# RWKV-6 attention and a SoLU feed-forward on one core: v and w_in loaded in bf16 by rounding transfers from GpSimd's queue, and a new order

## The chip, the core and the metric

The kernel runs on one core of a Trainium2 chip. The core has a matrix engine (TensorE, PE in the profile), VectorE (DVE), ScalarE (ACT), GpSimd (POOL, called Pool here) and SyncE (SP), which only issues transfers. Transfers are carried out by 16 engines that all queues share. The metric is the time of one execution on the device in microseconds, over several runs; the profile shows one execution more closely.

## The reference

Four sequences of 768 tokens, eight heads of 48 channels. The attention keeps a state of 48 by 48 per head, which decays by w at each token; its output goes through a feed-forward part with 1,024 hidden channels.

```python
for t in range(S):
    cur = einsum('bhd,bhe->bhde', u[None] * k_t, v_t)
    y[:, :, t] = einsum('bhd,bhde->bhe', r_t, state + cur)
    state = w_t[:, :, :, None] * state + einsum('bhd,bhe->bhde', k_t, v_t)
x = y.transpose(0, 2, 1, 3).reshape(B * S, H * D)          # 3072 x 384
h = x @ w_in                                               # 3072 x 1024
solu = h * softmax(h)
ln = (solu - mean(solu)) / sqrt(var(solu) + 1e-6) * g_ln
out = ln @ w_out                                           # 3072 x 384
```

All inputs and the output are float32.

## The kernel before

A unit is 128 tokens of one sequence: six chunks of four sequences, 24 units, numbered so that the four sequences of a chunk follow one another. Each unit passes through the same stages, and the whole program is written out by the string `ORDER`: each word is a stage, the unit's number and, after a dot, the engine or the PSUM slot (`LV3.a`: load v of unit 3 from ScalarE's queue; `kr5.d`: copy by VectorE). Every engine issues its own instructions in the order of these words; the class `InOrder` holds them to it. All its calls go through one line, so nearly every row of the profile carries L89 and is told apart by its tile.

The stages of a unit, by the words of `ORDER`, with the tile's name in the profile:

- Loads of w, k, r, v (`LW`, `LK`, `LR`, `LV`): each 128 partitions x 8 heads x 48 float32, 192 KB, in pieces of 192 bytes. Rings of seven buffers take w, k, r and v as float32. `LI` and `LO` load w_in (three parts of 512 KB) and w_out (two of 768 KB), `LU` and `LG` the vectors u and g.
- Decays: logarithm of w (`lw`, ScalarE), two cumulative products by triangular constants (`cum`, TensorE, tile cum_ps), exponent (`ex`, ScalarE), scaled k and r (`kp`, VectorE).
- The token's own term: `p` = k r and `q` = p u (Pool), their sum per head `dg` (VectorE), `dv` = v dg (Pool, tile dv). `vb` casts v to bf16, by Pool or ScalarE.
- Attention: k and r transposed (`krk`, `krr`, TensorE, tile kr_ps) and copied (`kr`), scores (`M`, tile m_ps), copied and masked (`m` on VectorE does both; `m` on ScalarE is followed by `sel`, Pool's mask), the attend product (`Y`, tile y_ps: from the state, and from masked scores and v; with `i` it also adds dv through an identity product, with `n` VectorE adds dv in `y`), and the state (`S`, `et`, `st`).
- Feed-forward: y transposed (`X`, `xT`, tile x_ps), hidden product (`H`, 24 products, tile h_ps), `e` = exp(h) (ScalarE), `he` = h e (VectorE), `hq` = he squared, the output product in two parts (`Oa`, `Ob`, tile o_ps: 384 columns and one for the mean in one product, and two single columns for the sum of e and of hq), then the factor from the sums (`sq`, `qm`, `lv`: ScalarE, VectorE, ScalarE), the scaling (`o`) and the store (`out`, SP).
- Once: u spread over the partitions (`us`, `uc`), g turned into a column (`gs`, `gc`), w_in cast to bf16 (`wi`), w_out scaled by g (`gw`) and centred (`mn`, `mc`, `ce`). `hot` are warm-up products without use.

The stages `KD` and `XD` transpose k and r, or y, by a transfer; the order before has none of them. The transfer queues are SP and ScalarE: `queue = {"s": sp, "a": act}`. A load waits in its queue for a free buffer of its ring, and everything behind it in that queue waits too.

Of the kernel before, what the change touches and what calls it, by code (L numbers as in the profile page):

```python
# [21 lines left out]
LW0.a LK0.s LU0.a LR0.s LW1.a LW2.s hot4.s3 LG0.s LK1.s lw0 LV0.a cum0.b0 LR1.s us0.s0 ex0 hot2.s3 uc0 lw1 LV1.s  # L22
p0 kp0 LW3.a LK2.a LR2.s krk0.s3 q0 krr0 cum1.b1 kr0.a hot2.s2 LV2.s LK3.a M0.b0 LR3.s p1 gs0.s1 ex1 m0.d
hot3.s3 LI1.s lw2 q1 dg0 cum2.b0 lw3 hot2.s3 kp1 vb0.p LI0.a S0.s2 dv0 vb1.a dg1 hot1.s3 ex2 Y0.is0 et0 LV3.a
cum3.b1 LI2.s p2 kp2 krk1.s3 gc0 LO0.s ex3 st0 LW4.s krk2.s1 q2 krr1 LO1.s krr2 kp3 kr1.a hot3.s2 dv1 LK4.s
kr2.d y0.a p3 M1.b0 LK5.a S1.s2 dg2 krk3.s3 vb2.a m1.d krr3 et1 wi0.a S2.s0 wi1.p M2.b1 st1 X0.s1 kr3.a m2.d
Y1.is2 LR4.s wi2.p et2 y1.a M3.b0 xT0.d LV4.a X1.s3 q3 m3.d H0.b1 dv2 gw1.a dg3 gw2.d e0 Y2.is2 LW5.s xT1.d
gw3.p st2 H1.b0 y2.a he0 lw4 gw0.a X2.s1 LR5.s e1 gw7.d cum4.b1 gw4.d hot2.s3 gw6.d gw5.d ex4 he1 vb3.p mn0.s3
LW6.s LV5.a dv3 xT2.a LK6.s kp4 S3.s0 mc0 Y3.is2 LR6.s lw5 ce6.d krk4.s1 ce3.d hq0.a cum5.b0 ce4.d krr4 ce2.d
H2.b1 ce7.d ex5 LW7.s ce1.d ce5.d ce0.d y3.a LK7.s p4 kp5 et3 Oa0.s3 lw6 e2 LR7.s kr4.d p5 krk5.s2 cum6.b0 st3  # L30
hq1.a Ob0 vb4.p he2 LW8.s q4 krr5 ex6 S4.s1 LK8.s kr5.d sq0 M4.b1 lw7 Oa1.s0 kp6 et4 m4.a LR8.s X3.s2 qm0 st4
vb5.p M5.b0 xT3.a cum7.b1 dg4 sel4 lv0 krk6.s1 LV6.s Ob1 m5.d ex7 LW9.s dv4 lw8 S5.s2 kp7 o0.a krr6 LK9.s p6
cum8.b0 sq1 et5 Y4.ns3 kr6.d ex8 H3.b1 q5 LV7.s y4.d hq2.a kp8 q6 LR9.s krk7.s1 e3 X4.s3 st5 LW10.s vb6.p M6.b0
krr7 xT4.d Oa2.s2 dg5 m6.a LK10.s qm1 kr7.d dv5 krk8.s3 lv1 Ob2 he3 out0 sel6 o1.a lw9 M7.b0 out1 dg6 S6.s1 sq2
m7.a LV8.s hq3.d krr8 cum9.b1 LR10.s Y5.ns0 vb7.p qm2 kr8.d lv2 H4.b0 p7 LW11.s et6 y5.d ex9 st6 p8 lw10 kp9
LV9.s X5.s3 S7.s0 e4 Oa3.s1 q7 o2.d vb8.a he4 out2 cum10.b1 dv6 xT5.a krk9.s2 et7 LK11.s ex10 Y6.ns3 q8 krr9 st7
LV10.s H5.b0 hq4.a kp10 sel7 LR11.s kr9.a y6.d M8.b1 dg7 LW12.s S8.s0 lw11 m8.d Ob3 dv7 et8 e5 LV11.s vb9.p
krk10.s3 st8 X6.s2 LK12.s p9 M9.b1 he5 xT6.a Y7.ns0 sq3 m9.a krr10 LR12.s S9.s2 dg8 cum11.b0 et9 LW13.s y7.d
H6.b1 lw12 dv8 ex11 kr10.d LK13.s p10 qm3 lv3 kp11 Oa4.s0 LR13.s e6 q9 st9 X7.s3 cum12.b0 LW14.s xT7.a Ob4 he6
p11 ex12 LV12.s krk11.s2 sel9 sq4 Y8.ns3 o3.a kp12 H7.b1 hq5.a out3 vb10.p qm4 y8.d q10 LK14.s lv4 dg9 M10.b0 e7  # L40
Oa5.s1 LR14.s m10.d vb11.p q11 o4.a krr11 LW15.s X8.s3 lw13 dg10 Ob5 p12 xT8.a out4 he7 kr11.a S10.s0 dv9 S11.s3
LV13.s dg11 sq5 hq6.a Y9.ns2 vb12.p qm5 cum13.b0 y9.d dv10 LK15.s H8.b1 et10 ex13 st10 LR15.s et11 lw14 kp13
Oa6.s2 LW16.s e8 hq7.d krk12.s0 lw15 M11.b0 p13 st11 LK16.s Ob6 lv5 he8 o5.a q12 krr12 m11.a Y10.ns3 out5 kr12.d
krk13.s1 cum14.b1 LR16.s y10.d sq6 krr13 sel11 ex14 cum15.b0 LW17.s kr13.d Oa7.s0 ex15 qm6 LV14.s kp14 p14
Y11.ns3 lw16 X9.s1 Ob7 kp15 lv6 dv11 LK17.s vb13.a xT9.d p15 o6.a M12.b1 y11.d M13.b0 m12.a X10.s1 out6 m13.d
krk14.s2 q13 S12.s3 LR17.s hq8.a krr14 H9.b1 dg12 LV15.s vb14.p xT10.d sq7 q14 et12 qm7 st12 LW18.s lv7 krk15.s1
dg13 e9 X11.s3 sel12 H10.b0 o7.d kr14.a out7 he9 dv12 LK18.s Y12.ns0 xT11.a p16 krr15 LR18.s Oa8.s2 e10 y12.d
kr15.d q15 LV16.s cum16.b1 he10 S13.s0 ex16 dv13 Ob8 LV17.s et13 kp16 q16 X12.s3 LW19.s Y13.ns1 sq8 xT12.a st13
M14.b0 vb15.p M15.b1 LK19.s m14.a y13.d krk16.s3 S14.s0 hq9.d krr16 LR19.s m15.a S15.s1 p17 qm8 kr16.d H11.b0
LW20.s et14 dg14 lv8 sel14 st14 et15 LK20.s dg15 H12.b1 e11 vb16.p o8.d sel15 st15 out8 lw17 Oa9.s3 he11 LV18.s  # L50
e12 vb17.p dv14 S16.s0 LV19.s hq10.a he12 Ob9 dv15 LR20.s et16 cum17.b0 st16 q17 Y14.ns2 LV20.s ex17 X13.s1
y14.d M16.b1 sq9 Oa10.s0 lw18 kp17 LW21.s m16.a Y15.ns2 qm9 xT13.d LK21.s cum18.b0 hq11.d lv9 krk17.s1 lw19
H13.b1 LR21.s o9.d p18 vb18.a dg16 ex18 LV21.s y15.d dv16 krr17 e13 Ob10 kp18 LW22.s sel16 X14.s3 hq12.a kr17.d
S17.s2 LK22.s cum19.b0 q18 he13 Oa11.s1 xT14.a LR22.s ex19 p19 X15.s3 lw20 M17.b1 out9 xT15.d Ob11 sq10 kp19
vb20.p m17.a LW23.s q19 Y16.ns3 qm10 dg17 et17 vb19.a cum20.b0 p20 LV22.s y16.d lv10 H14.b1 dg18 sq11 ex20 sel17
LK23.s st17 lw21 o10.d LR23.s Oa12.s3 e14 kp20 dv17 krk18.s2 Ob12 out10 hq13.a p21 qm11 he14 krk19.s0 LV23.s
lv11 krr18 q20 cum21.b0 sq12 o11.d krr19 ex21 H15.b1 p22 qm12 kr18.d out11 lv12 kr19.d vb21.p Oa13.s1 dv18 kp21
# [12 lines left out]
"""  # L70

NIO, NLW, NKP, NWK = 7, 10, 6, 4


class InOrder:


    def __init__(self, tc, engine):
# [18 lines left out]
def kernel(  # L97
# [80 lines left out]
    one_col = consts.tile([C, 2], BF16)  # L178
    dve.memset(one_col, 1.0)
    inv_col = consts.tile([C, 1], BF16)  # L180
    dve.memset(inv_col, 1.0 / RDF)
    ones_row = consts.tile([1, C], F32)
    dve.memset(ones_row, 1.0)

# [371 lines left out]
```

The softmax here doesn't subtract the row's maximum and nothing guards it: scores larger than these inputs give would overflow.

## Time and profile before

| | us |
|---|---|
| median of two runs | 154.74 (154.55 to 154.93) |
| profiled execution | 153.27 |
| its span, first to last instruction | 151.6 |
| busy: TensorE | 137.2 (91%) |
| VectorE | 127.9 (84%) |
| ScalarE | 117.9 (78%) |
| Pool | 94.9 (63%) |
| read from memory, written | 22.03 MB, 4.72 MB |

The span is what the profile covers; the execution is 1.7 us longer. A profile row names the line, the engine, the operation, what is written and read with sizes, the count; then the total busy time in us and the mean of one in ns; then the idle time of the engine ahead of these instructions, and who ended it. Buffer numbers are left out, so vb stands for all ten vb buffers. A matrix product's length is modelled and overlaps the next, so a row's mean is longer than the pace at which products follow each other; the pace is read from the chain. A DMA issue row shows how long the queue held the issuing engine, not how long the bytes took.

### The profile page before, as it was taken

To read this page: it belongs to the slowest core of one execution; us is meant where nothing else is said; L and a number is where in the kernel's file an instruction comes from. 1 tells how busy PE (TensorE), PEld (TensorE's weight loads), DVE (VectorE), ACT (ScalarE), POOL (GpSimd) and SP (SyncE) were. 2 spreads that over 40 slices of the span, in tenths; PEclk is the share of its full clock that TensorE was granted. 3 is DMA by queue.
4 is the path that set the end of the run, shared out by engine and by line. 5 is a ranking of instruction groups with operands and counts; after the bars stand their busy time and mean duration, and the time that the engine had idled before them with its cause. 6 is when DMAs were issued, how large, how long until landed. Compare 5 with 4: busy or idle time off the path is not lost.

```text
span 151.6 us, 5258 instructions
## 1 busy us (share of the span) xinstructions
PE 137.2 (91%) x2156; PEld 106.6 (70%) x2158; DVE 127.9 (84%) x235; ACT 117.9 (78%) x238; POOL 94.9 (63%) x127
## 2 busy tenths in 40 slices
PE   4799787879999997999988999999999999999980
PEld 1145566467788776888777797878887888889650
DVE  5209797999999996999976999999998998688940
ACT  3465766599999997999798688999898997484442
POOL 7484993531879859993849999299847682500000
PEclk9999999999999999999999999999999999999997
DMA  5999999999983999989699999898950111011142
GB/s 110 259 257 334 405 335 255 178 210 188 224 179 121 229 217 193 215 176 241 142 243 208 230 175 232 162 230 193 248 164 6 52 56 52 4 52 56 52 160 104
DMA packets 104825, 27.08 MB, mean 179 GB/s; under 512 B 100313, under 2 KB 104418, under 8 KB 104802
## 3 DMA queue, kind: packets, MB, share of 16 engines
q1 hardware_dynamic: 94256, 24.26, 69.6%
q10 hardware_dynamic: 10546, 2.49, 7.3%
q8 instruction: 17, 0.28, 0.7%
q14 instruction: 6, 0.05, 0.1%
HBM read 22.03 MB, written 4.72 MB: 176 GB/s over the span
## 4 chain that ended last, share of the span: by engine, by line
PE 54%; DMA 12%; SPq 10%; DVE 8%; ACT 6%; POOL 4%; issue 4%; ACTq 0%; POOLq 0%
PE o_ps L89 22%; PE h_ps L89 13%; SPq L89 10%; DMA w_in<-in_w_dram 6%; PE kr_ps L89 4%; PE y_ps L89 4%; DMA kr_in<-in_r_dram 4%; PE s_ps L89 3%; PE cum_ps L89 3%; PE m_ps L89 3%; DMA v_in<-in_v_dram 3%; PE x_ps L89 2%; DVE he L89 1%; POOL m L89 1%; DVE w L89 1%
## 5 line engine op out<-in xcount | busy, mean ns | idle before, releaser
L89 PE MATMUL o_ps<-w,he 128*128 128x385 bf16 x192 | 45.7, 325 | 0.1
L89 PE MATMUL h_ps<-xT,win_sb 128*128 128x128 bf16 x576 | 35.9, 219 | 0.3 <-DVE xT L89 0.3
L89 PEld LDWEIGHTS <-win_sb 128*128 128x128 bf16 x576 | 33.0, 98 | 0.9 <-issue 0.4
L89 PE MATMUL o_ps<-inv_col,e 128*128 128x1 bf16 x192 | 31.7, 165 | 0.0
L89 DVE TENSOR_TENSOR he<-h_ps,e 128x1024 bf16<-128x1024 f32 x24 | 29.1, 1216 | 2.7 <-ACT e L89 2.5
L89 PE MATMUL o_ps<-one_col,hq 128*128 128x1 bf16 x192 | 31.3, 163 | 0.0
L89 ACT ACTIVATE e<-h_ps 128x1024 bf16<-128x1024 f32 x24 | 24.5, 1020 | 4.7 <-PE h_ps L89 4.6
L89 DVE TENSOR_TENSOR kp<-cum_ps,kr_in 128x768 bf16<-128x768 f32 x24 | 22.7, 948 | 5.9 <-ACT cum_ps L89 5.6
L89 PEld LDWEIGHTS <-hq 128*128 128x128 bf16 x192 | 18.5, 96 | 12.8
L89 POOL TENSOR_TENSOR p<-kr_in 128x384 bf16<-128x384 f32 x24 | 24.4, 1018 | 3.7 <-DMA kr_in<-in_r_dram 3.6
L89 POOL TENSOR_TENSOR dv<-vb,dg 128x384 bf16<-128x384 bf16 x24 | 19.8, 830 | 9.6 <-DVE dg L89 7.4
L89 POOL TENSOR_SCALAR_AFFINE_SELECT m<-m 128x1024 bf16<-128x1024 bf16 x15 | 16.8, 1120 | 13.4 <-ACT sq L89 5.8
L89 POOL TENSOR_TENSOR q<-p,u_bc 128x384 bf16<-128x384 bf16 x24 | 21.8, 911 | 1.9 <-ACT u_bc L89 1.7
L89 PEld LDWEIGHTS <-kp 128*128 128x128 bf16 x272 | 17.4, 98 | 6.0 <-DVE kp L89 2.1
L89 ACT ACTIVATE cum_ps<-cum_ps 128x768 f32<-128x768 f32 x24 | 19.2, 802 | 3.0 <-PE cum_ps L89 2.9
L89 PE MATMUL kr_ps<-ident,kp 128*128 128x128 bf16 x192 | 18.0, 222 | 2.3 <-ACT gr L89 0.8
L89 PEld LDWEIGHTS <-he 128*128 128x128 bf16 x192 | 18.4, 96 | 0.9
L89 PEld LDWEIGHTS <-e 128*128 128x128 bf16 x192 | 18.4, 96 | 0.5 <-issue 0.2
L89 ACT ACTIVATE lw<-w_in 128x384 bf16<-128x384 f32 x24 | 12.4, 523 | 4.1 <-DMA w_in<-in_w_dram 4.1
L89 ACT CAST m<-m_ps 128x1024 bf16<-128x1024 f32 x15 | 15.0, 1013 | 0.7 <-PE m_ps L89 0.6
L89 DVE TENSOR_TENSOR m<-m_ps,keep 128x1024 bf16<-128x1024 f32 x9 | 10.9, 1215 | 4.2 <-PE m_ps L89 4.2
L89 ACT ACTIVATE hq<-he 128x1024 bf16<-128x1024 bf16 x13 | 13.7, 1057 | 0.0
(82 smaller groups left out, 262.5 us busy)
## 6 DMA issues: line engine op xcount, KB each, us to landing
kr_in<-in_r_dram SPq DMA_DIRECT2D x24, 192.0 KB, 4.3
out_dram<-o SPq DMA_DIRECT2D x24, 192.0 KB, 3.2
kr_in<-in_k_dram SPq DMA_DIRECT2D x21, 192.0 KB, 3.5
w_in<-in_w_dram SPq DMA_DIRECT2D x21, 192.0 KB, 4.2
v_in<-in_v_dram SPq DMA_DIRECT2D x20, 192.0 KB, 4.1
wout_f<-in_moe_w_out_dram SPq DMA_DIRECT2D x2, 768.0 KB, 7.7
win_f<-in_moe_w_in_dram SPq DMA_DIRECT2D x2, 512.0 KB, 5.1
v_in<-in_v_dram ACTq DMA_DIRECT2D x4, 192.0 KB, 4.2
```

The lines of the kernel that those rows point to most:

```text
L89: made = make(*args, **kwargs)
```

## The change

v and the three parts of w_in are loaded straight into bf16 tiles by transfers that Pool issues; the float32 buffers and the 24 + 3 casts are gone, and vb has rows of 64 as the other loads have. Pool's queue also takes ten of the 24 stores, ScalarE's the left half of the last one. SP issues all other loads but four at the start. In units 20 to 23, k and r, and y, are transposed by transfers that SP issues (`KD`, `XD`). The last unit's exponent, product and square are done in two parts, its three sums are computed ahead of its columns, and its columns in two halves (`Mal`, `Mar`, `Mbl`, `Mbr`) that VectorE and ScalarE scale and two queues store. The constants are filled by VectorE in a stage `pc` that stands behind the first three loads of v; Pool keeps four selections; `keep` is the same tile as `uts`. u is rounded to bf16 ahead of its spread. Ten instead of fifteen masks are Pool's, and two centrings. The words stand in a new order throughout.

```diff
@@ ORDER @@
-LW0.a LK0.s LU0.a LR0.s LW1.a LW2.s hot4.s3 LG0.s LK1.s lw0 LV0.a cum0.b0 LR1.s us0.s0 ex0 hot2.s3 uc0 lw1 LV1.s
-p0 kp0 LW3.a LK2.a LR2.s krk0.s3 q0 krr0 cum1.b1 kr0.a hot2.s2 LV2.s LK3.a M0.b0 LR3.s p1 gs0.s1 ex1 m0.d
-hot3.s3 LI1.s lw2 q1 dg0 cum2.b0 lw3 hot2.s3 kp1 vb0.p LI0.a S0.s2 dv0 vb1.a dg1 hot1.s3 ex2 Y0.is0 et0 LV3.a
-cum3.b1 LI2.s p2 kp2 krk1.s3 gc0 LO0.s ex3 st0 LW4.s krk2.s1 q2 krr1 LO1.s krr2 kp3 kr1.a hot3.s2 dv1 LK4.s
-kr2.d y0.a p3 M1.b0 LK5.a S1.s2 dg2 krk3.s3 vb2.a m1.d krr3 et1 wi0.a S2.s0 wi1.p M2.b1 st1 X0.s1 kr3.a m2.d
-Y1.is2 LR4.s wi2.p et2 y1.a M3.b0 xT0.d LV4.a X1.s3 q3 m3.d H0.b1 dv2 gw1.a dg3 gw2.d e0 Y2.is2 LW5.s xT1.d
-gw3.p st2 H1.b0 y2.a he0 lw4 gw0.a X2.s1 LR5.s e1 gw7.d cum4.b1 gw4.d hot2.s3 gw6.d gw5.d ex4 he1 vb3.p mn0.s3
...
-sq21 qm20 qm21 lv20 Oa23.s2 lv21 o20.d o21.d out20 Ob22 out21 Ob23 sq22 qm22 lv22 sq23 qm23 o22.d lv23 out22
-o23.a out23
+LV0.p LV1.p LV2.p pc0 LW0.s LG0.a LU0.s LK0.a hot5.s3 LW1.s LR0.s LW2.s gs0.s0 LK2.s lw0 ur0 LK1.a cum0.b0
+us0.s3 LR1.a hot1.s2 ex0 LR2.s lw1 LW3.s kp0 p0 uc0 cum1.b1 LK3.s lw2 krk0.s2 q0 ex1 krr0 cum2.b0 hot3.s3 ex2
+kp1 p1 LW4.s kr0.d krk1.s1 q1 LR3.s kp2 M0.b1 p2 dg0 LK4.s lw3 krk2.s3 krr1 m0.d krr2 dv0 kr1.a cum3.b0 LR4.s
+S0.s2 q2 dg1 gc0 Y0.is1 LO0.s lw4 kr2.d LI0.p S1.s0 ex3 cum4.b1 dv1 hot2.s3 LO1.s et0 y0.a kp3 LW5.s ex4 p3 dg2
+M1.b0 LK5.s krk3.s3 st0 LI1.p X0.s1 m1.d S2.s2 LR5.s LI2.p dv2 kp4 M2.b0 krr3 LV3.p kr3.a m2.d xT0.a q3 krk4.s3
+gw0.a krr4 Y1.is1 et1 LV4.p gw1.d kr4.a dg3 M3.b1 m3.d y1.a p4 et2 X1.s3 Y2.ns1 xT1.d M4.b0 q4 st1 m4.a H0.b1
+gw3.d LV5.p y2.d gw2.a st2 H1.b0 e0 dg4 LW6.s gw7.d gw6.d gw4.a gw5.d S3.s3 dv3 he0 e1 X2.s0 mn0.s1 LK6.s sel4
+lw5 he1 xT2.a LR6.s Y3.is2 et3 mc0 dv4 cum5.b1 st3 H2.b0 ex5 LW7.s LV6.p ce3.d ce6.d y3.a ce1.d ce5.d LK7.s lw6
+S4.s0 kp5 p5 e2 X3.s1 Y4.ns3 LR7.s xT3.d ce2.p cum6.b1 hq0.a he2 S5.s2 LW8.s krk5.s1 ce7.p et4 ex6 krr5 y4.d
...
+M22.b0 y21.d M23.b1 m22.a Oa18.s0 m23.d XD21 sq17 hq19.a H20.b0 sel22 qm17 out16 et19 lv17 dv23 st19 Y22.ns1 e20
+Y23.ns3 y22.d Ob18 y23.d o17.a XD22 he20 H21.b1 out17.p XD23 Oa19.s1 e21 H22.b0 sq18 hq20.a he21 Ob19 hq21.d
+Ha23.b1 qm18 sq19 lv18 Oa20.s3 e22 o18.d qm19 out18.p Hb23 ea23 he22 Ob20 eb23 lv19 hq22.d Oa21.s2 sq20 o19.a
+heb23 Oa22.s0 out19 qm20 hqb23.d lv20 hea23 Ob21 hqa23.d Ob22 sq21 qm21 o20.d lv21 Sa23.s1 sq22 out20 qm22 o21.d
+Sb23 lv22 Mar23.s3 sq23 out21 Mal23.s2 qm23 o22.d lv23 Mbr23 Mbl23 out22 or23.d ol23.a outr23 outl23.a
@@ constants and buffers @@
-    v_t = ring("v_in", NIO, [C, H, 64], F32)
-    win_f = consts.tile([128, KM, DF], F32)
+    vb_t = ring("vb", NLW, [C, H, 64], BF16)
+    win_sb = consts.tile([128, KM, DF], BF16)
...
-    dve.memset(warm, 0.0)
     uti_neg = consts.tile([C, C], BF16)
-    pool.memset(uti_neg, -1.0)
-    pool.affine_select(out=uti_neg, in_=uti_neg, compare_op=ALU.is_ge, fill=0.0, base=0,
-                       pattern=[[1, C]], channel_multiplier=-1)
...
-    ones_row = consts.tile([1, C], F32)
+    ones_row = consts.tile([1, C], BF16)
...
-    vb_t = ring("vb", NLW, [C, H, D], BF16)
+    keep = uts
+
+    def constants(i, x):
+        dve.memset(warm, 0.0)
+        dve.memset(uti_neg, -1.0)
+        dve.memset(uts, 1.0)
+        dve.memset(ident, 0.0)
+        dve.memset(ident_f, 0.0)
+        pool.affine_select(out=uti_neg, in_=uti_neg, compare_op=ALU.is_ge, fill=0.0, base=0,
+                           pattern=[[1, C]], channel_multiplier=-1)
...
+        dve.memset(halves, 0.0)
+        dve.memset(off_blocks, 0.0)
+        for row, own in ((0, 0), (32, 1)):
+            dve.memset(halves[row:row + 1, 64 * own:64 * own + 64], 1.0)
+            dve.memset(off_blocks[row:row + 1, :, 1 - own], -30000.0)
...
-    queue = {"s": sp, "a": act}
+    queue = {"s": sp, "a": act, "p": pool}
@@ loads, u and the casts @@
     def load_v(i, x):
-        queue[x].dma_start(out=v_t[i % NIO][:, :, :D], in_=rows_of(v, i))
+        queue[x].dma_start(out=vb_t[i % NLW][:, :, :D], in_=rows_of(v, i))
...
     def load_w_in(j, x):
-        queue[x].dma_start(out=win_f[:, j, :], in_=moe_w_in[j * 128:(j + 1) * 128, :])
+        queue[x].dma_start(out=win_sb[:, j, :], in_=moe_w_in[j * 128:(j + 1) * 128, :])
...
+    def round_u(i, x):
+        dve.tensor_copy(out=u_b, in_=u_row)
+
     def spread_u(i, x):
         ps["u"] = bank([C, DM], F32, x, "u_ps")
-        pe.matmul(ps["u"], lhsT=ones_row, rhs=u_row, start=True, stop=True)
+        pe.matmul(ps["u"], lhsT=ones_row, rhs=u_b, start=True, stop=True)
...
-    def cast_w_in(j, x):
-        copy = {"a": act.copy, "d": dve.tensor_copy, "p": pool.tensor_copy}[x]
-        copy(out=win_sb[:, j, :], in_=win_f[:, j, :])
...
-    def v_cast(i, x):
-        copy = {"a": act.copy, "p": pool.tensor_copy}[x]
-        copy(out=vb_t[i % NLW], in_=v_t[i % NIO][:, :, :D])
@@ the last unit @@
-    def hidden(i, x):
-        xT = xT_t[i % NWK]
-        h_ps = live[i]["h_ps"] = bank([128, KF, C], F32, x, "h_ps")
-        for f in range(KF):
+    def hidden_part(i, f0, f1):
+        xT, h_ps = xT_t[i % NWK], live[i]["h_ps"]
+        for f in range(f0, f1):
             for j in range(KM):
...
+    def hidden_a(i, x):
+        live[i]["h_ps"] = bank([128, KF, C], F32, x, "h_ps")
+        hidden_part(i, 0, KF // 2)
...
+    def hidden_exp(i, x, part=ALL):
+        act.activation(out=e_t[i % NWK][:, part], in_=live[i]["h_ps"][:, part], func=EXP)
...
+    HALF = {"l": slice(0, DM // 2), "r": slice(DM // 2, DM)}
+
+    def columns_of(i, x, side, part):
+        if part == 0:
+            live[i]["o" + side] = bank([C, DM // 2], F32, x, "o_ps")
+        for f in range(part * KF // 2, (part + 1) * KF // 2):
+            pe.matmul(live[i]["o" + side], lhsT=he_t[i % NWK][:, f, :], rhs=w2[:, f, HALF[side]],
+                      start=(f == 0), stop=(f == KF - 1))
+
+    def sums_of(i, x, part):
+        if part == 0:
+            live[i]["sums"] = bank([C, 3], F32, x, "o_ps")
+        to = live[i]["sums"]
+        for f in range(part * KF // 2, (part + 1) * KF // 2):
+            pe.matmul(to[:, 0:1], lhsT=he_t[i % NWK][:, f, :], rhs=w2[:, f, DM:], start=(f == 0), stop=False,
+                      skip_group_check=True)
...
-    def scaled_out(i, x):
-        o_ps, rs, o = live[i]["o_ps"], rs_t[i % NWK], o_t[i % NWK]
+    def scaled_out(i, x, side=""):
+        rs, o = rs_t[i % NWK], o_t[i % NWK][:, HALF.get(side, slice(0, DM))]
...
-    def store(i, x):
+    def store(i, x, side=""):
         c, b = units[i]
-        sp.dma_start(out=out[b * S + c * C:b * S + (c + 1) * C, :], in_=o_t[i % NWK])
+        cols = HALF.get(side, slice(0, DM))
+        queue[x or "s"].dma_start(out=out[b * S + c * C:b * S + (c + 1) * C, cols], in_=o_t[i % NWK][:, cols])
```

## The prediction

> **What bounds the kernel now.** I read the time slices first, then the busy table by stage, then the chain of waits, then the groups. The slices (engine, busy tenths of 40 slices of 3.8 us):
>
> ```profile
> PE   4799787879999997999988999999999999999980
> POOL 7484993531879859993849999299847682500000
> DMA  5999999999983999989699999898950111011142
> ```
>
> Two things overlap: transfers are full until slice 29 (110 us), and TensorE is nearly full from slice 10 (38 us). The stages, cut at the first output product (34 us), the last load (110), Pool's last instruction (131) and TensorE's last (146.4); columns are named in the first line:
>
> ```profile
> core 0: us, PE busy (x) PEld busy (x) DVE busy (x) ACT busy (x) POOL busy (x), PEclk, DMA share, GB/s
> 0.00:34.00 34.00, 26.51 (x269) 15.65 (x272) 23.24 (x57) 20.84 (x38) 21.78 (x41) 1.00 1.07 261
> 34.00:110.00 76.00, 73.54 (x1261) 60.27 (x1259) 71.81 (x120) 68.95 (x141) 59.74 (x71) 1.00 0.96 202
> 110.00:131.00 21.00, 21.00 (x373) 17.55 (x372) 18.57 (x33) 18.52 (x35) 13.41 (x15) 1.00 0.19 59
> 131.00:146.40 15.40, 15.40 (x255) 12.60 (x254) 13.44 (x25) 7.74 (x21) 0.00 (x0) 1.00 0.16 59
> ```
>
> The first 34 us belong to the transfers (share 1.07, TensorE idle 7.5 us and 7.8 us of its busy time are warm-up products, rows of 7.2 and 0.6). After that TensorE sets the pace: idle 2.5 us in 76, then not at all. Pool is free 21% of the middle and ends 20.7 us before the span. The end, from the chain of waits (start, length, what):
>
> ```profile
> 135.65 0.17 PE x_ps L89 x3
> 135.82 0.83 PE o_ps L89 x12
> 136.65 0.19 PE x_ps L89 x3
> 136.84 1.34 PE h_ps L89 x24
> ...
> 140.38 5.98 PE o_ps L89 x84
> 146.38 0.18 ACT sq L89
> ...
> 148.20 0.58 ACT o L89
> ```
>
> These lengths are TensorE's real pace: 1.34 us for a unit's hidden product, 0.83 for half its output product, 0.19 for three transposes; elsewhere in the chain 0.24 for four transposes of k or r. After the last product 5.2 us remain. The rows that the change touches on Pool and ScalarE, and one issue row (ns minimum, median, maximum):
>
> ```profile
> L89 POOL TENSOR_TENSOR p<-kr_in 128x384 bf16<-128x384 f32 x24 | 24.4, 1018 | 3.7 <-DMA kr_in<-in_r_dram 3.6
> L89 POOL TENSOR_TENSOR q<-p,u_bc 128x384 bf16<-128x384 bf16 x24 | 21.8, 911 | 1.9 <-ACT u_bc L89 1.7
> L89 POOL CAST vb<-v_in 128x384 bf16<-128x384 f32 x17 | 8.5, 502 | 6.1 <-DMA v_in<-in_v_dram 6.1
> L89 ACT CAST vb<-v_in 128x384 bf16<-128x384 f32 x7 | 3.6, 515 | 1.4 <-DMA v_in<-in_v_dram 1.3
> L89 ACTq DMA_DIRECT2D v_in<-in_v_dram x4: 374/374/379, 4.3 to 29.9; - x4
> ```
>
> **What the Trainium skill says.** "DMA: Bandwidth & Descriptors", section "SWDGE vs HWDGE vs iDMA": a transfer that changes the type can only be issued by GpSimd, whose own cores then write every descriptor. The trace before has no such transfer. Its section "Latency and other measured facts" gives about 1 us to the first byte on that path, named as the emission overhead, against 0.6 us for the hardware path; the 0.374 us above is the hardware issue alone. "SBUF — State Buffer", section "Who interferes with whom": GpSimd cannot write descriptors while VectorE runs an operation that takes both ports. No run here shows it, but VectorE is 94% busy in the middle. "Issuing engines are not separate DMA queues" (the first page): the bytes still share the same engines, so 1.07 and 0.96 are not relieved by another queue.
>
> **The change part by part.**
> *Casts gone.* 24 casts of v (8.5 us Pool, 3.6 us ScalarE) and three of w_in (2.0 Pool, 1.0 ScalarE). TensorE covers nearly all of it: only one v cast (0.48 us) lies on the chain. Worth at most 1 us.
>
> *Pool's new queue.* c is what one issue holds Pool. 24 loads of v, 3 of w_in and 10 stores make 37 issues, 35 ahead of the last dv. Lower bound of c 0.37 us (the row above). Upper bound: a v load has 128 x 8 = 1,024 pieces; if one costs Pool what an element of q costs, 911/384 = 2.4 ns, c is 2.4 us. I take the skill's 1.0. Pool's compute becomes 24 x (1.018 + 0.911 + 0.830, the last for dv) = 66.2, ten masks instead of fifteen at 1.12 = 11.2, two centrings at about 0.9 = 1.8, four constants 1.2: 80.4 us. After the last dv TensorE still has two attend products, and output and hidden products of units 18 to 23: 15.2 us at the paces above, and then the end, 3.2 us. With about 8 us in which Pool has nothing ready (an estimate: it was 3.7 before p and 1.9 before q, and dg comes late at the start), Pool's limit on the span is 80.4 + 8 + 15.2 + 3.2 + 35c = 106.8 + 35c: **141.8 at c = 1.0**, 151.6 (as now) at 1.28, 154.7 at 1.37, 190.8 at 2.4, 119.8 at 0.37. Queued behind each issue are p, q, dv and the mask; VectorE (dg, y) and TensorE (attend) wait for those. A store from Pool also waits for its scaled output, and holds them as long.
>
> *Transfers.* Bytes read are the same; 192 KB at 207 GB/s is 0.95 us of all engines. Rounding may save on the write (0.7) or run at half pace (1.9); I take 0.95, no effect. At 1.9, 24 loads add 23 us to engines that are full to 110 us.
>
> *TensorE.* Units 20 to 23 transpose k, r and x by transfer: 4 x (0.47 + 0.19) = 2.65 us gone, with their copies on ScalarE and VectorE. One more identity product, +0.33. The last unit's output product becomes 16 products of 192 columns (0.083 each, 1.33) and 24 single columns with a weight load each (0.055, as a transpose, 1.3) for 1.66: +1.0. Net **-1.3**. The transposing transfers lie on an idle stage (share 0.19). A store lands in 1.8 to 2.2 us there, a load under load in 4.1; between y and the hidden product stand 2.8 us of products, so the cost is 0 to 1.3, I take 0.
>
> *The end.* The sums come before the last columns, so squares, logarithm and exponent (1.8 us) lie beside 1.4 us of products, and the scaling (0.58) is split over two engines. **-2.0** (bounds -1.0 and -2.4).
>
> *The start.* By the order, TensorE now does four hidden products and six state products before the first output product, not three and four: 19.8 us of useful work at these paces against 15.9. If that output still began at 33.7 us this would be 3.8 us gained; but it needs V4, V5 and W6 landed too, about 27 loads instead of 22, in a stage that transfers bound. I take half, **-2.0** (bounds -3.8 and +3: three v issues now stand ahead of the constants that the first cumulative product reads, 3c, and w_in waits its turn behind seven Pool operations). The constants' fills move to VectorE, whose first product waited until 6.55 us: 0. The u spread in bf16 and eight fewer warm-up products lie in waits: 0. Loads moved from ScalarE's queue to SP's: 0, the engines are full either way.
>
> *The middle.* Of 2.5 us idle, with ScalarE rid of casts, **-1.0** (0 to -2.5).
>
> Sum: 1.3 + 2.0 + 2.0 + 1.0 = 6.3 off the profiled span of 151.6, so 145.3, which Pool's 141.8 stays under by only 3.5. The shown median, 154.74, is 3.1 above that span (the profiled execution itself took 153.27), so 148.4; I say **148**.
>
> **The rivals.**
> *Pool becomes the bound* (slower). It decides from c = 1.28; at 1.7 the limit is 166.3, the time 169. For it: 1,024 pieces written by software, VectorE's ports, in-order stores in Pool's queue. Against: the skill's 1 us, and 36 us of Pool's waiting before 131 us that could be filled. Chance 0.28.
> *Rounding slows the transfers* (slower): at 1.4 us a load, 24 x 0.45 = 11 us more until the last load, perhaps half of it shown after the gains: about 160. Chance 0.08.
> *Hidden anyway* (within 2%): the casts were covered, the casts' place on Pool is taken by issues at 1.2 us, Pool and TensorE limit each other and the gains at start and end go into waits: 153 to 156. Chance 0.12. That the change doesn't do what it says is excluded for the casts, which are no longer in the program; for w_in the late landing above would be it.
>
> **How the numbers follow.** Forecast 0.52, its own range 142 to 151.5 (the bounds of start, end and middle); rivals 0.28, 0.08, 0.12. Two per cent, about what a measurement tells from no change, is 151.6 and 157.8. Faster 0.50 (the forecast less its edge), same 0.14, slower 0.36. The range goes from 142 to 168: half of Pool's rival (c above 1.7) and 0.05 below lie outside.
>
> **What would show it.** Right: Pool's issue rows at 0.8 to 1.1 us, Pool's dv of unit 23 done by 126 us, TensorE without gaps from 34 us, under 3.5 us from its last product to the end, no cast rows. Wrong: attend products released by Pool's dv or mask all through the middle, Pool busy without a break, issue rows above 1.3 us (Pool's rival); v landing later than 5 us after issue and a DMA share near 1 beyond 115 us (rounding); a first output product after 36 us (start); hidden products of units 20 to 23 released by transfers (transposes).

## The result, and the profile after

The changed kernel took **163.62 us** (163.51 to 163.72, two runs) against 154.74: a ratio of 1.0574 (95% interval 1.0510 to 1.0638). The forecast was 148 us. Some executions of each of these kernels take one to three per cent longer than the rest, and the ratios below leave them out. The profiled execution took 163.51 us, its span is 161.8. The time slices of the changed kernel, now of 4.0 us (PEclk is the TensorE clock that was granted, in tenths):

```profile
PE   5637759796599999299999999999999998998990
POOL 7246999189841799990999956799977956140100
PEclk9999985589969999879999999999999999999999
DMA  5999999999999999789899299919999632132123
```

The slices are counted from 0. TensorE is still full from slice 17 on, but it gets there later, and it drops to 2 in slice 16 (65 us). Its granted clock is below nine tenths in slices 5 to 8 (20 to 36 us), in slice 11 (44 us) and again in slices 16 and 17. Pool fills 66% of the span (63 before): it did not become the engine without a gap that the first rival needs. Busy time by stage, cut at equal times, of the kernel before and then of the changed one:

```profile
core 0: us, PE busy (x) PEld busy (x) DVE busy (x) ACT busy (x) POOL busy (x), PEclk, DMA share, GB/s
0.00:30.00 30.00, 23.59 (x230) 13.28 (x232) 19.59 (x48) 17.13 (x29) 20.20 (x39) 1.00 1.07 267
30.00:50.00 20.00, 18.92 (x315) 15.20 (x311) 19.65 (x37) 19.16 (x39) 12.74 (x17) 1.00 0.90 186
50.00:100.00 50.00, 47.54 (x823) 39.19 (x819) 46.05 (x75) 44.08 (x89) 39.24 (x47) 1.00 0.98 205
100.00:140.00 40.00, 40.00 (x702) 33.93 (x701) 36.46 (x66) 33.01 (x67) 22.75 (x27) 1.00 0.38 97
140.00:162.00 22.00, 7.20 (x103) 4.97 (x100) 6.16 (x13) 4.49 (x16) 0.00 (x0) 0.91 0.15 54
```

```profile
0.00:30.00 30.00, 18.86 (x170) 10.94 (x172) 18.96 (x57) 14.27 (x25) 20.21 (x30) 0.89 1.17 197
30.00:50.00 20.00, 16.59 (x211) 14.10 (x208) 16.01 (x22) 13.02 (x23) 14.64 (x16) 0.83 1.41 180
50.00:100.00 50.00, 46.80 (x782) 37.56 (x781) 47.75 (x73) 42.94 (x85) 39.32 (x44) 0.97 1.11 173
100.00:140.00 40.00, 39.23 (x678) 32.07 (x676) 38.89 (x65) 32.82 (x68) 30.03 (x35) 1.00 0.79 131
140.00:162.00 22.00, 17.43 (x288) 14.11 (x287) 13.66 (x27) 12.07 (x33) 3.01 (x4) 1.00 0.28 88
```

Length less TensorE's busy time is its idle time, and these differences make up the whole loss: idle up to 50 us went from 7.5 to 14.6 (**+7.1**), from 50 to 140 from 2.5 to 4.0 (**+1.5**), from 140 to the end of the span it is 4.4 both times, and busy time grew from 137.25 to 138.90 (**+1.65**). Together 10.2 us, the 161.8 less 151.6 of the spans. The busy time holds the warm-up products, which lie in waits: 7.55 us before, 4.78 now. Without them it grew by 4.4 us, although the order has less work for TensorE. The chain of waits of the changed kernel shows where (start, length, what):

```profile
43.74 2.69 PE h_ps L86 x24
67.73 1.64 PE o_ps L86 x12
73.23 1.34 PE h_ps L86 x24
78.40 0.83 PE o_ps L86 x12
```

Behind each of its two longest waits, TensorE took twice its usual time for a hidden product or half an output product, while the granted clock was 0.83 (40 to 50 us) and 0.88 (60 to 70 us). So a wait here cost more than its own length. In the kernel before, the clock was 1.00 in every stage up to 140 us.

For whom TensorE waited, in the changed kernel (total, times, longest, us):

```profile
PE cum_ps L86 <- DVE kp L86: 3.4, 1, 3.4
PE o_ps L86 <- DVE st L86: 3.0, 1, 3.0
PE kr_ps L86 <- DVE kp L86: 2.3, 2, 2.1
PE cum_ps L86 <- ACT lw L86: 1.7, 2, 1.4
PE g_ps L86 <- POOL ident_f L86: 1.6, 1, 1.6
...
PE h_ps L86 <- DMA win_sb<-in_moe_w_in_dram: 1.1, 1, 1.1
```

The two longest are waits for VectorE, not for Pool or a transfer. The place of the second one, in the timeline (start, length, engine, line, operation):

```profile
62.35 0.55 DVE L86 TENSOR_TENSOR y<-y_ps,dv 128x384 bf16<-128x384 f32 x1
62.81 4.39 DVE L86 TENSOR_TENSOR hq<-he 128x1024 bf16<-128x1024 bf16 x1
67.13 0.55 DVE L86 TENSOR_TENSOR st<-s_ps,et 128x384 bf16<-128x384 f32 x1
...
61.28 1.83 POOL L86 DMA_DIRECT2D vb<-in_v_dram  x2
63.12 0.93 POOL L86 TENSOR_TENSOR q<-p,u_bc 128x384 bf16<-128x384 bf16 x1
64.00 1.62 POOL L86 TENSOR_TENSOR dv<-vb,dg 128x384 bf16<-128x384 bf16 x2
65.56 1.09 POOL L86 TENSOR_SCALAR_AFFINE_SELECT m<-m 128x1024 bf16<-128x1024 bf16 x1
...
67.73 0.48 PE L86 MATMUL o_ps<-w,he 128*128 128x385 bf16 x1 [3.04 <-DVE st L86]
```

The square `hq` of unit 4 took 4.39 us, where VectorE's squares have a median of 686 ns (in the kernel before 681, the longest 1,419). It ended 0.55 us after Pool's last operation of an unbroken row of q, two dv and a mask, and that row was unbroken because two issues of v (1.83 us) stood ahead of it. A second square, that of unit 17, took 2.8 us at 134 us. The other long wait is alike: four of VectorE's centring additions took 4.67 us from 36.75 on, beside Pool at work without a break, and kp behind them came late. In the kernel before, the eight additions (count, minimum/median/maximum in ns, first and last start) were:

```profile
L89 DVE TENSOR_TENSOR w<-w,mean_sb x8: 344/350/605, 31.2 to 33.3; 128x384 bf16<-128x384 bf16 x8
```

### The profile page after: what moved, and what is told of

Its sections match the earlier page's. It is cut to its first block, busy times and chain, and to the rows that moved or that the text cites. A ratio compares the mean times of both kernels' runs of the same rounds, so it can differ in the third digit from the quotient of the medians.

```text
span 161.8 us, 5193 instructions
## 1 busy us (share of the span) xinstructions
PE 138.9 (86%) x2121; PEld 108.8 (67%) x2122; DVE 135.3 (84%) x239; ACT 115.1 (71%) x232; POOL 107.2 (66%) x129
## 4 chain that ended last, share of the span: by engine, by line
PE 56%; DVE 14%; DMA 14%; issue 5%; SPq 4%; POOL 2%; ACT 2%; DVEq 0%; ACTq 0%; POOLq 0%
PE o_ps L86 20%; PE h_ps L86 17%; DMA win_sb<-in_moe_w_in_dram 5%; DMA kr_in<-in_r_dram 5%; DVE hq L86 4%; PE s_ps L86 4%; PE y_ps L86 4%; SPq L86 3%; PE cum_ps L86 3%; PE kr_ps L86 3%; PE m_ps L86 3%; DMA kr_in<-in_k_dram 2%; DVE w L86 2%; DMA xT<-y 2%; PE x_ps L86 2%
## 5 line engine op out<-in xcount | busy, mean ns | idle before, releaser
L86 PE MATMUL o_ps<-w,he 128*128 128x385 bf16 (+2 forms) x208 | 47.7, 319 | 3.1 <-DVE st L86 3.0
L86 PE MATMUL h_ps<-xT,win_sb 128*128 128x128 bf16 x576 | 39.6, 229 | 1.6 <-DMA win_sb<-in_moe_w_in_dram 1.1
L86 PEld LDWEIGHTS <-win_sb 128*128 128x128 bf16 x576 | 35.9, 103 | 3.0 <-DMA win_sb<-in_moe_w_in_dram 1.4
L86 DVE TENSOR_TENSOR he<-h_ps,e 128x1024 bf16<-128x1024 f32 (+1 forms) x25 | 29.4, 1175 | 6.0 <-ACT e L86 5.7
L86 ACT ACTIVATE e<-h_ps 128x1024 bf16<-128x1024 f32 (+1 forms) x25 | 24.6, 986 | 9.8 <-PE h_ps L86 9.5
L86 POOL TENSOR_TENSOR dv<-vb,dg 128x384 bf16<-128x384 bf16 x24 | 19.8, 831 | 11.1 <-DVE dg L86 7.3
L86 POOL DMA_DIRECT2D vb<-in_v_dram x23 | 21.3, 928 | 0.0
L86 PEld LDWEIGHTS <-he 128*128 128x128 bf16 x208 | 19.6, 97 | 1.0 <-DVE o L86 0.2
L86 PE MATMUL kr_ps<-ident,kp 128*128 128x128 bf16 x160 | 15.9, 232 | 3.4 <-DVE kp L86 2.3
L86 DVE TENSOR_TENSOR m<-m_ps,uts 128x1024 bf16<-128x1024 f32 x14 | 17.0, 1217 | 1.5 <-PE m_ps L86 1.5
L86 ACT ACTIVATE hq<-he 128x1024 bf16<-128x1024 bf16 x17 | 17.9, 1056 | 0.3 <-DVE he L86 0.3
L86 POOL TENSOR_SCALAR_AFFINE_SELECT m<-m 128x1024 bf16<-128x1024 bf16 x10 | 10.9, 1090 | 10.9 <-ACT m L86 6.2
```

Of the source, the lines that this page charges most:

```text
L86: made = make(*args, **kwargs)
```

## The experiments

Each ratio is against the kernel before, run on the same chip in the same comparison; times of different comparisons are not set against each other.

| run | ratio (95% interval) |
|---|---|
| old_order_round | 1.0207 (1.0159 to 1.0255) |
| old_win_round | 1.0260 (1.0193 to 1.0328) |
| new_plain_pool | 1.0460 (1.0379 to 1.0541) |
| new_plain_sp | 1.0161 (1.0102 to 1.0221) |
| new_all_sp | 1.0375 (1.0320 to 1.0430) |
| after_again | 1.0474 (1.0405 to 1.0543) |
| new_hq4_act | 1.0261 (1.0149 to 1.0372) |
| new_win_early | 1.0624 (1.0515 to 1.0733) |
| new_start | 1.0369 (1.0253 to 1.0485) |
| new_less_v | 1.0491 (1.0424 to 1.0558) |
| new_no_lock | 1.0230 (1.0155 to 1.0305) |
| new_no_lock_sp | 1.0186 (1.0112 to 1.0259) |
| new_no_transpose | 1.0847 (1.0766 to 1.0929) |
| old_tail | 0.9920 (0.9879 to 0.9961) |
| old_turn | 0.9923 (0.9893 to 0.9953) |

### Is it the rounding, Pool as issuer, or the order?

Three theories at first: rounding costs the transfer engines (1), any transfer that Pool issues is dear (2), the new order and its start lose (3).

**loads_alone** leaves the computation out: the 24 loads of v three times over, rounded by Pool, plain by Pool, plain by SP.

> The loads by themselves; the computation is left out. In order: 24 loads of v rounded by Pool's transfers, the same 24 by Pool without rounding (float32 to float32), the same 24 by SP, then the three parts of w_in rounded by Pool, and the same by SP as float32. Each group ends before the next starts. In the changed kernel a packet of Pool's queue took 33 ns of an engine (33.2% of 16 engines x 161.8 us over 26,032 packets), one of SP's 19 ns. Theory 1 (rounding is what costs the engines): about 2.0 us a load rounded, about 1.1 in both float32 groups. Theory 2 (any transfer whose descriptors Pool writes is dear): 2.0 us in both of Pool's groups, 1.1 on SP. Theory 3 (only the order and the start are at fault): all three groups within 10% of each other, at 1.1 us.

The timeline of this run has all 24 rounding issues in a row, and the first reader of what they brought:

```profile
1.27 21.16 POOL L38 DMA_DIRECT2D oneb<-in_v_dram  x24
25.13 1.03 POOL L38 CAST marks<-oneb 128x1 f32<-128x1 bf16 x8 [2.70 <-DMA oneb<-in_v_dram]
```

0.88 us an issue, and a load every 1.0 us (23.9 us for 24). Plain, a load took 1.3 us from Pool's queue and 1.28 from SP's. Rounding loads move no slower; theory 1 falls for loads by themselves.

**new_plain_pool, new_plain_sp**: the changed kernel with v in float32, its products and dv reading the upper half of each element (v is truncated, not rounded).

```diff
-    vb_t = ring("vb", NLW, [C, H, 64], BF16)
+    vb_t = ring("vb", NLW, [C, H, 64], F32)
+    def v_of(i):
+        return vb_t[i % NLW].bitcast(BF16)[:, :, 1:2 * D:2]
```

> The new order, with v loaded from Pool's queue without rounding: float32 tiles, and the products and dv read the upper half of each float32 as a bf16 value (v truncated instead of rounded), so that no cast is needed. Nothing else is changed; w_in is still rounded. Theory 1: the engines' work falls by about 20 us, 150 to 157 us. Theory 2: 161 to 165 us. Theory 3: 161 to 165 us.

> As the run before, but the float32 loads of v are issued by SP at the same places of the order, so Pool has 24 issues of 0.93 us less. Theory 1: 148 to 156 us, within 2 us of the run before. Theory 2: 148 to 156 us, where the run before stays at 161 to 165. Theory 3: 159 to 165 us.

Pool or SP as issuer of the same bytes makes 3% (1.046 against 1.016); rounding, by comparison with the changed kernel, is not resolved. From the output product of unit 3 to that of unit 6 the changed kernel needs 24.0 us, new_plain_pool 24.0, new_plain_sp 19.4, the kernel before 19.6: the 4.5 us between the two runs lie in this stretch. There the square of unit 4 took 4.37 us in new_plain_pool and 1.01 us in new_plain_sp.

**old_order_round, old_win_round**: the kernel before, its order kept, with v alone or w_in alone rounded by Pool and the casts gone.

```diff
-vb0.p LI0.a ... LV3.a
+LI0.a ... LV3.p
```

> The order of before, with one part of the change: v is loaded rounded from Pool's queue at the places where it was loaded before, and the 24 casts of v are gone; w_in and all else as before. Theories 1 and 2: the transfers' work grows by about 23 us (24 x 0.95), the last load lands well after 120 us instead of 110, and the time is 159 to 168 us. Theory 3: 152 to 156 us.

> The kernel before with one part of the change: the three parts of w_in loaded in bf16 by rounding transfers from Pool's queue, at the same words, its three casts gone; v as before. Theory E: the first hidden product from 21.8 to 25 us or later, the time 1.5 to 3 us longer, ratio 1.01 to 1.02. Theory D: within 1 us of the kernel before, ratio 0.993 to 1.007.

Each loses over 2%, without the new order; but old_order_round, at 156.0 us, lies at the edge of what theory 3 allowed (152 to 156) and below the 159 that theories 1 and 2 asked for. What the move of v changed at the start shows in the timeline of old_order_round:

```profile
7.27 1.90 SPq L89 DMA_DIRECT2D win_f<-in_moe_w_in_dram  x2
...
18.09 0.96 DVE L89 TENSOR_TENSOR kp<-cum_ps,kr_in 128x768 bf16<-128x768 f32 x1 [3.79 <-DMA kr_in<-in_k_dram]
```

With the loads of v out of its queue, SP came to the 512 KB parts of w_in at 7.27 us instead of 10.23, and k, 192 KB and needed sooner, landed behind them: issued by ScalarE at 7.75 us, it took 10.2 us. kp waited 3.79 us, and TensorE 4.1 for kp. This wait is not the whole loss: by 100 us TensorE had idled 10.5 us, hardly more than before (9.95), and 1.8 us of the 2.7 by which the profiled span grew is longer busy time, at a granted clock of 0.95 and less up to 140 us. In old_win_round SP came to w_out at 10.22 instead of 12.22, while Pool issued w_in. The next load of w took 10.0 us to land, ScalarE waited for it ahead of a cast of v, and TensorE waited for that cast; here idle time up to 100 us did grow, by 3.0 us, and busy time by 1.6.

```profile
PE s_ps L89 <- ACT vb L89: 3.5, 1, 3.5
```

A load moved to another queue advances all that stood behind it in the old one.

### VectorE beside Pool

**after_again, new_hq4_act**: the changed kernel unaltered, and with one word, `hq4.d`, changed to `hq4.a`.

> The changed kernel itself, as the yardstick of this comparison. Expected 162 to 164 us, ratio 1.05 to 1.06. What it tells is whether the two losses seen in the first profile come back: hq of unit 4 on VectorE at about 4.4 us beside a Pool that issues and computes without a break, and the first output product at about 46.5 us. If the long hq is an accident of one execution, it is not there again.

> The changed kernel, the square of unit 4 (hq4) on ScalarE instead of VectorE: one word. Theory A (VectorE's operation with two inputs from SBUF is held up by Pool's unbroken work, and this one stall stands on the chain): 3 to 4.5 us less than the changed kernel, 159 to 160.5 us, and the stretch from the output product of unit 3 to that of unit 6 goes from 24.1 to about 20. Theory B (the stretch is long because v of these units is late, or Pool itself is): within 1 us of the changed kernel, the stretch stays at 23 to 24.

The long square is no accident: 4,396 ns again. Without it the stretch from unit 3 to unit 6 is 19.8 us instead of 24.1, and the time 3.3 us less (161.3 and 158.0, the means that enter the ratios; same comparison, and the intervals are apart). This one square on VectorE is 2.1 of the 4.7 points that the changed kernel loses here.

**ports_alone** leaves the computation out: six squares beside six of each kind of Pool operation.

> The computation is left out: VectorE's square hq (two inputs from SBUF, 128 x 1024 bf16) six times beside six of Pool's p, of its q, of its mask, of its issues of v, each pairing by itself; then twelve VectorE copies of 128 x 384 (one input) beside six q; then hq alone. Theory A (a two-input VectorE operation gets no turn while Pool works without a break on SBUF): beside q and the mask the first hq takes as long as all six Pool operations, 5 to 7 us, then 0.68 each; the copies are not held up. Beside the issues: 0.68 each if writing descriptors takes no port, longer if it does. Rival (they share in turns): each hq about 1.5 us beside q, and Pool's operations lengthened too.

Groups by tile in this run (count, minimum/median/maximum in ns, first and last start): hq beside p, beside q, beside the mask, beside issues of v, and alone; then the copies beside q.

```profile
L38 DVE TENSOR_TENSOR hq<-he x6: 1471/1478/1480, 4.5 to 11.5; 128x1024 bf16<-128x1024 bf16 x6
...
L38 DVE TENSOR_TENSOR hq<-he x6: 1304/1390/1391, 13.4 to 19.9; 128x1024 bf16<-128x1024 bf16 x6
...
L38 DVE TENSOR_TENSOR hq<-he x6: 1479/1572/1573, 21.7 to 29.1; 128x1024 bf16<-128x1024 bf16 x6
...
L38 DVE TENSOR_TENSOR hq<-he x6: 680/684/685, 31.0 to 34.1; 128x1024 bf16<-128x1024 bf16 x6
...
L38 DVE TENSOR_TENSOR hq<-he x6: 680/684/685, 43.5 to 46.6; 128x1024 bf16<-128x1024 bf16 x6
...
L38 DVE COPY xT<-xs x12: 246/564/1055, 36.6 to 42.9; 128x384 bf16<-128x384 bf16 x12
```

A square beside Pool's operations takes about twice its 0.68 us, and they lengthen too (q from 0.91 to 1.35). The Trainium skill, "SBUF — State Buffer", section "Who interferes with whom", says it: a VectorE instruction with two inputs from SBUF contends with a GpSimd instruction that reads SBUF, and the lock holds for a whole instruction. Issues of v neither hold the square up nor suffer (0.91 us). In this run the engines took turns, so theory A is half wrong: one operation is waited for, not all. The copies, which I had expected free, were held up too (564 ns, 246 at best). In the kernel one square waited through four Pool operations, more than turns explain. The section also says that whoever issues first holds the lock; there the square was due at 62.90 us, when VectorE's operation before it ended, q began at 63.12, and q went first. The measurement decides; its reason isn't settled.

**new_no_lock, new_no_lock_sp**: the changed kernel, and new_plain_sp, with the squares of units 4 and 17 on ScalarE and VectorE's centring in one group that reads the mean from PSUM, so that none has two SBUF inputs there.

```diff
-hq4.d ... hq17.d ... ce5.d LK7.s ... ce4.d et5 kr5.a ce0.d
+hq4.a ... hq17.a ... ce5.d ce4.d ce0.d LK7.s ... et5 kr5.a
-        (dve if x == "d" else pool).tensor_add(out=w2[:, f, :DM], in0=w2[:, f, :DM], in1=mean_sb)
+        (dve if x == "d" else pool).tensor_add(out=w2[:, f, :DM], in0=w2[:, f, :DM],
+                                               in1=ps["mean"] if x == "d" else mean_sb)
```

> The changed kernel with every VectorE operation taken away that reads two inputs from SBUF beside a busy Pool and was long there: the squares of units 4 and 17 on ScalarE, and VectorE's six centring additions reading the mean from PSUM, in one group. Rounding transfers, order and transposes stay. Theory A (VectorE held up beside Pool is the larger half of the loss): the first output product at 42 to 43.5 us instead of 44.8, the stretch from unit 3's output product to unit 6's at 19.5 to 20, in all 4.5 to 6 us less than the changed kernel (161.3 in its comparison), ratio 1.01 to 1.02. If only the square counts, as in new_hq4_act: ratio 1.026.

> new_plain_sp (v as float32 by SP, read through its high halves, truncated) with the same three edits. If what v from Pool costs is only that it fills Pool's gaps beside VectorE, the gain here is small and the two kernels of this pair meet: ratio 1.005 to 1.012 against 1.016 of new_plain_sp, and new_no_lock within 1 us of it. If the issues by Pool or the rounding have a cost of their own, new_no_lock stays 2 us or more above this one.

New_no_lock is at 1.023, clear of the changed kernel's 1.047 with Pool issuing and rounding as before, and within the other's interval: beyond VectorE's waits, v from Pool costs nothing that can be told within these intervals (0.7% to either side). But it is not clear of new_hq4_act (1.026), so what the other square and the centring add can't be told either. Its first output product came at 44.2 us, where 42 to 43.5 were expected and after_again had 44.8; and new_no_lock_sp gained nothing on new_plain_sp (1.019 against 1.016). Groups and stages of new_no_lock:

```profile
L86 DVE TENSOR_TENSOR w<-w,mean_ps x6: 547/549/553, 37.5 to 39.9; 128x384 bf16<-128x384 bf16 x6
```

```profile
0.00:30.00 30.00, 20.18 (x166) 11.42 (x168) 18.46 (x55) 14.15 (x25) 20.25 (x30) 0.91 1.16 198
30.00:50.00 20.00, 18.55 (x258) 15.56 (x256) 16.56 (x28) 15.02 (x30) 14.37 (x16) 0.88 1.41 172
50.00:100.00 50.00, 49.73 (x858) 40.54 (x855) 47.73 (x81) 47.59 (x92) 43.99 (x50) 1.00 1.20 194
```

An addition from PSUM is slower (549 ns against a median of 350 in the kernel before) but takes 549 each time, though Pool works beside it. In one group the six still held TensorE up once, for 1.3 us. TensorE's idle time from 30 to 50 us is 1.45 instead of 3.4, from 50 to 100 us 0.3 instead of 3.2. The first 30 us stay bad: 9.8 us idle (11.1 in the changed kernel, 6.4 before).

### The start

**new_win_early, new_start, new_less_v, new_all_sp**: w_in right behind p of unit 0; the constants and w, k, r of unit 0 ahead of the three loads of v; no loads of v for units 3 to 6, which read v of units 0 to 2 (the computation is changed); and new_plain_sp with w_in too as float32 from SP, truncated.

```diff
-kp0 p0 uc0 ... LI0.p ... LI1.p ... LI2.p
+kp0 p0 LI0.p LI1.p LI2.p uc0
```

```diff
-LV0.p LV1.p LV2.p pc0 LW0.s LG0.a LU0.s LK0.a hot5.s3 LW1.s LR0.s LW2.s
+pc0 LW0.s LK0.a LR0.s LG0.a LU0.s LV0.p hot5.s3 LW1.s LV1.p LV2.p LW2.s
```

```diff
-LV3.p ... LV4.p ... LV5.p ... LV6.p
+        return vb_t[(i - 3) % 3 if 3 <= i <= 6 else i % NLW]
```

> The changed kernel, the three loads of w_in issued right behind p of unit 0 on Pool instead of some twelve operations later. Theory C (the start loses because w_in's issue waits in Pool's queue): H of unit 0 at about 22 us instead of 28, the first output product at 40 to 42 instead of 46.5, the time 3 to 5 us less, 158.5 to 160.5. Theory D (the start is bound by the transfers of everything, w_in only changes places with another load): the first output product within 1.5 us of 46.5, the time within 1 us of the changed kernel or above it.

> The changed kernel, its first words in another order: the constants and the loads of w, k, r of unit 0 ahead of the three loads of v on Pool. Theory C2 (the first r and the constants come late, and this delays everything behind them): p of unit 0 at 5 to 6 us instead of 9.4, the first output product 3 to 4 us earlier, the time 2 to 4 us less. Theory D (transfers bound the start): p0 earlier, but the first output product within 1.5 us of 46.5 and the time within 1 us.

> The changed kernel without the loads of v of units 3 to 6, whose products read v of units 0 to 2 again (so the computation is changed): 0.79 MB and four of Pool's issues less ahead of the first output products, nothing else. Theory D (bytes bind the start of the new order): at 207 GB/s 3.8 us less transfer, the first output product 3 to 4 us earlier than 44.8, and the time 2 to 4 us less than the changed kernel, 157.5 to 159.5. Rival (the start loses by waits between the engines, VectorE and Pool above all, not by bytes): first output product within 1.5 us, time within 1 us.

> The changed kernel with v and w_in not rounded: both issued by SP as float32, at the same places of the order, and read through the high halves of each element (truncated instead of rounded). Against new_plain_sp only w_in differs. Theory E (w_in through Pool's queue is what makes the start late): the first output product at 38 to 41 us instead of 44.6, ratio 0.98 to 1.00. Theory D (the new order needs more bytes before its first output product, whoever issues them): the first output product within 1.5 us of 44.6, ratio 1.01 to 1.02.

Four edits, and the first output product stays where it was or comes later: 44.8 us in after_again, 46.0, 45.1, 45.4, and in new_all_sp 47.5 against 44.6 of new_plain_sp. w_in issued at once made the decays' loads late (ScalarE waited 10.2 us for w, 6.0 in after_again). In new_all_sp SP's full queue let the last part of w_in out only at 27.4 us. 0.79 MB less changed nothing, so at least these bytes do not bind this start. Theory D had fitted new_win_early and new_start; it falls here and in new_all_sp, where its ranges were missed too, and C, C2 and E fall with it. Only new_start may give something (1.037 against 1.047, intervals overlapping). What TensorE idles in the first 30 us is spread over waits of 1 to 2 us each: for the first r and k, for the logarithm, for g's constant behind the issues of v, for w_in. Which of them sets the rest isn't settled, and no run here changes the clock by itself.

### The parts counted as gains

**new_no_transpose**: the changed kernel with TensorE's transposes again in units 20 to 23. **old_tail**: the kernel before with the last unit's sums ahead and its columns in halves. **old_turn**: old_tail with the transposing transfers. **old_turn_plain**: old_turn with v in float32, truncated, without casts.

```diff
-KD20 ... XD20
+krk20.s0 krr20 kr20.a ... X20.s0 xT20.d
```

```diff
-Oa23.s2 ... Ob22 out21 Ob23 sq22 qm22 lv22 sq23 qm23 o22.d lv23 out22 o23.a out23
+Ob22 out21 Sa23.s2 sq22 qm22 Sb23 lv22 Mar23.s3 sq23 Mal23.s1 qm23 o22.d lv23 Mbr23 Mbl23 out22 or23.d ol23.a outr23 outl23.a
```

> The changed kernel with k, r and y of units 20 to 23 transposed by TensorE and copied by ScalarE and VectorE again, as in the other units, in place of the transposing transfers. As predicted (the transfers save 2.65 us of TensorE on the path): 2 to 2.7 us more than the changed kernel, 163.5 to 165. Rival (the hidden products then wait for the transfers of y, and TensorE has gaps in the tail anyway): within 1 us of the changed kernel, or below it.

> The kernel before with one part of the change: the last unit's sums ahead of its columns, the columns in two halves, scaled by two engines and stored by two queues (its exponent, product and square stay whole). As predicted (1.0 us more of TensorE, 2.0 us less after the last product): 1.0 us less, ratio 0.992 to 0.995, and 3.2 us from the last product to the end instead of 4.4. Rival (the extra column products cost what the end saves): ratio 0.998 to 1.004.

> The kernel before with two parts of the change that the predicted sum counted as gains: the last unit's sums and columns in halves (as in old_tail), and k, r and y of units 20 to 23 transposed by transfers. Its own order, its own loads and casts. As predicted (TensorE 2.65 us less for the transposes, the transfers hidden): ratio 0.97 to 0.978. Rival (TensorE waits for the transposed y, whose landing takes 2.4 us and more): ratio 0.985 to 0.995, no better than old_tail.

> old_turn with the casts of v gone and nothing put in their place: v loaded as float32 from the same queues as before and read through the high halves of each element (truncated instead of rounded). As predicted for the casts (at most 1 us on the path): ratio 0.000 to 0.007 below old_turn. If reading every second element slows the products or Pool's dv, it is above old_turn.

Taking the transfers away raised the ratio by 3.7 points, 5.7 us where 2 to 2.7 were expected, and more than the 2.3 us by which TensorE's busy time grew (136.98 to 139.28); the rest may come from where I put the words, which no run shows. In the order before they bring nothing (0.9923 against 0.9920): TensorE's busy time falls to 135.49 from 137.25, and idle time takes its place, 0.9 us of it from 110 to 130 us where there was none. The last unit's halves give 1.2 us (0.6 to 1.9 by the interval); 3.2 us remain after the last product, where 4.4 remained before. Old_turn_plain's six runs lie between 151.54 and 158.86 us, too scattered for a ratio; nothing follows from it. Nothing tried beats the kernel before by 2%.

## Why the prediction was wrong

**The start, −2.0.** This step failed. The first output product came at 46.5 us instead of 33.7. Less the 3.9 us of work that the order puts ahead of it, that is 8.9 us lost, far outside the bounds (−3.8 and +3). The prediction took the stage as bound by transfers and asked how many bytes are needed; new_less_v shows that 0.79 MB less don't bring the product forward. Two things stand in its place. TensorE idled 7.1 us more up to there, in waits between engines that had no term in the sum; the longest, for VectorE's centring beside Pool, is 3.4 us in the first profile and 2.1 in after_again. And its products took longer: without warm-up products its busy time up to there grew from 19.0 to 27.2 us, 4.3 more than the 3.9 of added work (an estimate, from the profiles and the prediction's own count). Which wait has to go to mend the start stays open: new_no_lock, with the additions from PSUM, brought the product only from 44.8 to 44.2 us.

**The middle, −1.0.** This step failed too. It became +1.5: the casts' time came back, but one square took 4.39 us, and TensorE, behind it, waited 3.0 us and then ran slowly. The prediction named VectorE's ports from the same section of the skill, but for the wrong pair: descriptors held up by VectorE. No run shows that; the case is Pool's reads against VectorE's second input, and the trace before held its victims (hq at 1,419 ns once, an addition at 605). new_hq4_act takes this square away, and 2.1 of the 4.7 points go with it.

**Pool's issue, c = 1.0.** Right for v (0.93 us), too high for w_in (0.60) and a store (0.59). Pool's last dv ended at 142.8 us, not by 126: up to there Pool was idle for 36.8 us, as it had been before (36), where the limit of 141.8 allowed 8. The rival that makes Pool the bound from c = 1.28 did not come; what Pool's work cost was time on another engine.

**Transfers, "no effect".** Right as to the pace of rounding, which loads_alone shows, and wrong as to landing: w_in took 8.0 us instead of 5.1. "0, the engines are full either way" for loads moved from ScalarE's queue to SP's was not tested by itself. The two runs in the old order, which moved other loads, speak against it: what stood behind the moved loads was issued earlier, and a small load landed late.

**TensorE, −1.3.** Not confirmed. Busy time fell by 1.3 us in new_plain_sp (135.95 against 137.25), but warm-up products make 2.55 us of this (7.55 and 5.00), so that the rest rose by 1.25: the agreement is luck. In the profiled changed kernel the rest rose by 4.4, with a granted clock of 0.89 and 0.83 in the first two stages, before 1.00. The clock was not in the sum.

**The end, −2.0.** This term was mis-sized from the start. The 5.2 us after the last product were counted from the sum `sq` at 146.38 us, which belongs to unit 22; the last product of the kernel before ended at 147.2, and 4.4 remained. In the changed kernel it is 3.7: a gain of 0.7, outside the bounds (−1.0 to −2.4). The mechanism holds, since in old_tail 3.2 us remain. For the transposed y TensorE waited 0.5 us, within the bounds.

Of the rivals none is what happened: rounding does not slow transfers, nothing was hidden, Pool did not bind. The signs listed told rightly what failed: a first output product after 36 us (46.5), and gaps in TensorE after 34 us.

## What to carry to other kernels

When an engine is given more work, list what shares a port with it: here each VectorE operation with both inputs in SBUF that stands near a busy Pool. Move it to ScalarE before Pool's gaps are filled, which gave 2.1 points here for one square, or let it read PSUM, which made the additions even but whose gain in time was not told apart. When a load changes queue, write down what its old queue will now issue earlier, and which small, urgent load lands behind it. An operation saved where TensorE is not what ends last gives its time to idle, as the transposes did in the old order. In a forecast, take warm-up products out of TensorE's busy time, and leave room for slower products behind a long wait.

## What the hardware showed unexpectedly

- A square of 0.68 us took 1.3 to 1.6 us beside Pool's operations in ports_alone, but 4.39 us in the kernel, much the same in every profile of the new order in which Pool issued v, rounded or not, and this square was VectorE's (4.15 to 4.41); copies with one input were held up too.
- Issues of v ran beside those squares without harm to either (0.91 and 0.68 us).
- TensorE's granted clock between 20 and 30 us was 0.51 to 0.96 in the runs of the new order, 0.75 and 0.66 in old_order_round and old_win_round, and 1.00 in the kernel before and old_turn. How busy TensorE was in the ten microseconds ahead doesn't tell which: 8.1 us in old_turn (1.00 after it), 8.4 in new_plain_sp (0.66).
- Behind waits of 3.4 and 3.0 us, 24 hidden products took 2.69 us instead of 1.34, and 12 products of an output 1.64 instead of 0.83; behind the wait of 2.1 us in after_again the hidden products kept their pace.
- Rounded loads of v alone landed every 1.0 us, plain ones every 1.28.
